# Loading one K tile in four with a transposing DMA in a two-block cached attention kernel

## The chip, the cores and the metric

The kernel runs on one core of a Trainium2 chip. A core has five engines that run their own instruction streams: PE (TensorE, matrix multiply), DVE (VectorE), ACT (ScalarE), POOL (GpSimd) and SP (SyncE, here used only to issue DMAs), and 16 DMA engines that move data between HBM and the on-chip memory. PE writes its results to PSUM; DVE and ACT empty PSUM into SBUF. Engines wait for one another by semaphores.

The metric is the device time of one execution in microseconds.

## The reference

Two independent blocks, A and B, of the same shape; each projects queries, attends over a cache, projects the result, and the two outputs are concatenated:

```python
# B, Sq, D = 16, 64, 640;  H, Sk, Dh = 32, 512, 128;  all bfloat16
q = (x @ wq).reshape(B, Sq, H, Dh).transpose(0, 2, 1, 3)
scores = jnp.einsum("bhqd,bhkd->bhqk", q, k_cache) * (Dh ** -0.5)
p = softmax(scores, axis=-1)
o = jnp.einsum("bhqk,bhkd->bhqd", p, v_cache)
out = o.transpose(0, 2, 1, 3).reshape(B, Sq, H * Dh) @ wo
```

K and V of one batch element and head are 512 x 128 each, 128 KB. Over both blocks they are 134 MB each, and nearly all that the kernel reads.

## The kernel before

**Work units.** A step g is one head for two batch elements: 2 x 64 query rows fill the 128 partitions. A macro m is two neighbouring heads (steps 2m and 2m+1, called sub 0 and 1); there are 256 macros. Index j names the batch element of the pair. Eight macros (16 heads) of one pair form a group; a pass runs all eight pairs through 16 heads of one block, and there are four passes. A chunk is two macros (four heads), the unit of the K and V loads.

**Stages of a macro**, with the names that the code uses:

- KX (PE, L433): eight 128x128 transposes of a K tile (two heads of one j, 2 x 512 keys x 128) into one PSUM bank, KTB. There are two per macro, j = 0 and 1 (KX0, KX1).
- KE (DVE, L442): copies that bank to ktp_ring, in the score matmul's layout. KE0 and KE1 use the same bank, so a KX waits for the KE before it.
- QP2 (PE, L451): queries of two heads; QE2 (ACT, L459) scales and empties them.
- SM2 (PE, L467): four score matmuls, sub by j, into two PSUM banks; it waits for KE1 and for the EX that emptied the banks.
- MX (DVE, L476), EX (ACT, L482): negated row maximum and exponential with row sum, once per sub. RC2 (DVE, L488): reciprocals of the row sums.
- NM (POOL, L496): normalises P into pn_ring, once per sub.
- TR2 (PE, L505): eight transposes of P; TE2 (DVE, L512) empties them.
- PV2 (PE, L524), OE2 (ACT, L532), OP2 (PE, L540 and L545): P times V, emptying, output projection, accumulated over the 16 heads.
- Once per group: XT and XE (PE L604, ACT L612) transpose the next x. The accumulated output goes to outp (OVP, ACT, L555) in the first pass of a block and is added to it (OVF, DVE, L560) in the second; the store follows.

**Order.** The order on each engine is written out as a template per iteration, with an offset that says how many macros ahead each stage works:

```python
PE_T = (("TR2", 1), ("QP2", 4), ("KX", 4, 0), ("SM2", 3), ("PV2", 1), ("XT", 0), ("OP2", 0), ("KX", 4, 1))
DVE_T = (("TE2", 1), ("RC2", 2), ("KE", 4, 0), ("MX", 3, 0), ("MX", 3, 1), ("KE", 4, 1), ("OVF", 0))
POOL_T = (("NM", 0, 0), ("NM", 0, 1))
```

In iteration k, PE thus transposes K of macro k+4, multiplies scores of k+3, transposes P of k+1 and projects the output of k. An engine works strictly in its order. Dependencies are found from what each operation reads and writes; a pruning pass removes waits that another wait implies.

**Loads.** All loads go through SP's queue in one planned order (L229 to L240). Each has a time from which its buffer is free and a due time, in units of iterations; the planner steps through time with an assumed duration of each load (DMA_NS) and always takes the free load with the earliest due time. When the program runs, SP waits at each load for the real semaphore of its buffer. K goes into kn_ring and V into v_ring, both five chunks deep. Per chunk and j there is one K load of 512 KB (L626): 128 partitions, each row of 2 KB holding eight neighbouring keys (t = 8) of one head. V is loaded likewise (L622) with four keys, 1 KB, a row. Weights wq and wo have two buffers by pass, x has one.

Of the kernel before, what the change touches and what calls it, by code (L numbers as in the profile page):

```python
# [5 lines left out]
BF16 = mybir.dt.bfloat16  # L6
# [8 lines left out]
class Cfg:  # L15
    G = 4
    HH = 16
    NKB = 5
# [13 lines left out]
    DVE_T = (("TE2", 1), ("RC2", 2), ("KE", 4, 0), ("MX", 3, 0), ("MX", 3, 1), ("KE", 4, 1), ("OVF", 0))  # L32
    POOL_T = (("NM", 0, 0), ("NM", 0, 1))
    TAIL_SPLIT = 2
    SLOT_NS = 3600.0
    DMA_NS = dict(LDK=3100.0, LDV=3100.0, LDWQ=3900.0, LDWO=4300.0, LDX=700.0)


class Op:
# [3 lines left out]
    def __init__(self, eng, kind, idx, reads=(), writes=(), dur=0.0, ts=None, aux=None):  # L43
        self.eng = eng
        self.kind = kind
        self.idx = idx
        self.reads = tuple(reads)
        self.writes = tuple(writes)
        self.sem = None
        self.count = None  # L50
        self.deps = []
        self.waits = []
        self.dur = dur
        self.ts = ts
        self.aux = aux
        self.dma = kind in ("LDK", "LDV", "LDX", "LDWQ", "LDWO", "ST")


STAGES = ("LDW", "LDX", "LDK", "LDV", "KX0", "KE0", "KX1", "KE1", "QP2", "QE2", "SM2", "MX0", "MX1", "EX0", "EX1",
          "RC2", "NM0", "NM1", "TR2", "TE2", "XT", "XE", "PV2", "OE2", "OP2", "OV", "ST")  # L60
STAGE_IDX = {s: i for i, s in enumerate(STAGES)}
SUB_KINDS = ("KX", "KE", "EX", "NM", "MX")
# [2 lines left out]
def build_plan(dims, cfg):  # L65
# [22 lines left out]

    progs = {e: [] for e in ENGINES}

    def mk(eng, kind, idx, reads, writes, stage, m_ts, sub=0, aux=None, dur=0.0):
        return Op(eng, kind, idx, reads, writes, dur=dur, aux=aux, ts=(m_ts, STAGE_IDX[stage], sub))

# [4 lines left out]
    def make_op(kind, m, sub):  # L98
        g0, g1 = 2 * m, 2 * m + 1
        ps_, bp, grp, h0 = step_info(g0)  # L100
        c = g0 // G
        if kind == "KX":
            return mk("pe", "KX", (m, sub), [("kn", c % cfg.NKB, g0 % G), ("kn", c % cfg.NKB, g1 % G), ("ident",)],
                      [("KTB",)], "KX%d" % sub, m, sub)
        if kind == "KE":
            return mk("dve", "KE", (m, sub), [], [("KTB",), ("ktp", m % cfg.NKT, sub)], "KE%d" % sub, m, sub)
        if kind in ("MX", "EX", "NM"):
            g = 2 * m + sub
            r = g % cfg.NR
            if kind == "MX":  # L110
                return mk("dve", "MX", g, [], [("SB", sub), ("negmax", r)], "MX%d" % sub, m, sub)
            if kind == "EX":
                return mk("act", "EX", g, [("negmax", r)], [("SB", sub), ("p", g % cfg.NP), ("rowsum", r)],
                          "EX%d" % sub, m, sub)
            return mk("pool", "NM", g, [("p", g % cfg.NP), ("recip", r)], [("pn", g % cfg.NPN)], "NM%d" % sub, m, sub)
        r0, r1 = g0 % cfg.NR, g1 % cfg.NR
        if kind in ("XT", "XE"):
            mt = m + cfg.XLEAD
            if mt % MPG != 0 or not (0 <= mt < NMAC):
                return None  # L120
            gq = mt // MPG
            m_ts = mt - cfg.XLEAD + OFF["TR2"]
            if kind == "XT":
                return mk("pe", "XT", gq, [("xn", gq % cfg.NXN), ("ident",)], [("PTB",)], "XT", m_ts, aux=gq)
            return mk("act", "XE", gq, [], [("PTB",), ("xT", gq % cfg.NX)], "XE", m_ts, aux=gq)
        if kind == "QP2":
            return mk("pe", "QP2", m, [("xT", grp % cfg.NX), ("wq", ps_ % 2, h0 // G)], [("QB",)], "QP2", m)
        if kind == "QE2":
            return mk("act", "QE2", m, [], [("QB",), ("qT", m % cfg.NQ)], "QE2", m)
        if kind == "SM2":  # L130
            return mk("pe", "SM2", m, [("qT", m % cfg.NQ), ("ktp", m % cfg.NKT, 0), ("ktp", m % cfg.NKT, 1)],
                      [("SB", 0), ("SB", 1)], "SM2", m)
        if kind == "RC2":
            return mk("dve", "RC2", m, [("rowsum", r0), ("rowsum", r1)], [("recip", r0), ("recip", r1)], "RC2", m)
        if kind == "TR2":
            return mk("pe", "TR2", m, [("pn", g0 % cfg.NPN), ("pn", g1 % cfg.NPN), ("ident",)], [("PTB",)], "TR2", m)
        if kind == "TE2":
            return mk("dve", "TE2", m, [], [("PTB",), ("pT", m % cfg.NT)], "TE2", m)
        if kind == "PV2":
            return mk("pe", "PV2", m, [("pT", m % cfg.NT), ("v", c % cfg.NVB, g0 % G), ("v", c % cfg.NVB, g1 % G)],  # L140
                      [("OB",)], "PV2", m)
        if kind == "OE2":
            return mk("act", "OE2", m, [], [("OB",), ("oT", m % cfg.NO)], "OE2", m)
        if kind == "OP2":
            return mk("pe", "OP2", m, [("oT", m % cfg.NO), ("wo", ps_ % 2, h0 // G)], [("OUTB",)], "OP2", m)
        if kind in ("OV", "OVF", "ST"):
            if h0 + 1 != SPB - 1:
                return None
            last_half = ps_ % NHALF == NHALF - 1
            if kind == "OV":  # L150
                if NHALF == 1:
                    return mk("act", "OV", m, [], [("OUTB",), ("out_sb", grp % 2)], "OV", m, aux=grp)
                if last_half:
                    return None
                return mk("act", "OVP", m, [], [("OUTB",), ("outp", bp)], "OV", m, aux=grp)
            if kind == "OVF":
                if NHALF == 1 or not last_half:
                    return None
                return mk("dve", "OVF", m, [("outp", bp)], [("OUTB",), ("out_sb", grp % 2)], "OV", m, aux=grp)
            if NHALF == 1 or not last_half:  # L160
                return None
            return mk("act", "ST", m, [("out_sb", grp % 2)], [("out_dram", grp)], "ST", m, aux=grp)
        raise ValueError(kind)
# [57 lines left out]
    for c in range(NCHUNK):  # L221
        m0 = MPC * c
        for kind, ring, n_ring, cons, tb in (("LDK", "kn", cfg.NKB, "KX", 2), ("LDV", "v", cfg.NVB, "PV2", 2.5)):
            ready = NEG if c < n_ring else MPC * (c - n_ring + 1) - 1 - OFF[cons]
            for pi, (piece, j, hlo, hhi) in enumerate(chunk_pieces(c)):
                op = mk("sp", kind, (c, j, piece), [], [(ring, c % n_ring, gi) for gi in range(hlo, hhi)], kind,
                        m0, aux=(c, j, hlo, hhi, piece), dur=cfg.DMA_NS[kind] * (hhi - hlo) / 8.0)
                loads.append((ready, m0 - OFF[cons] + 0.01 * hlo, tb + 0.001 * pi, op))
    pending = sorted(loads, key=lambda e: (e[1], e[2]))  # L229
    t_now = min(e[1] for e in loads) - 4.0  # L230
    while pending:
# [12 lines left out]
    def sem_key(op):  # L244
        if op.kind in ("LDK", "LDV"):
            return ("d_" + op.kind[2:].lower(), op.writes[0][1], op.aux[4])
        if op.kind == "LDX":
            return ("d_x", op.writes[0][1])
        if op.kind in ("LDWQ", "LDWO"):
# [97 lines left out]
def mha_kernel(nc, blocks, out, cfg=None):  # L347
# [30 lines left out]
    with contextlib.ExitStack() as es:  # L378
# [7 lines left out]
        outp = sb("outp", [128, NBP, DN], F32) if NHALF > 1 else None  # L386
        xT_ring = sb("xT_ring", [128, NX, KT, 128], BF16)
        xn_ring = sb("xn_ring", [128, NXN, D], BF16)
        kn_ring = sb("kn_ring", [128, NKB, 2, G // 2, 8, DH], BF16)
        v_ring = sb("v_ring", [128, NVB, 2, G, 4, DH], BF16)  # L390
        ktp_ring = sb("ktp_ring", [128, NKT, 2, 2, SK], BF16)
        qT_ring = sb("qT_ring", [128, NQ, 2, 128], BF16)
# [34 lines left out]
        def em_KX(e, op):  # L427
            m, j = op.idx
            g0 = 2 * m
            c, hp = g0 // G, (g0 % G) // 2  # L430
            first = last = None
            for t8 in range(8):
                ins = e.transpose(kt_ps[:, t8, :], kn_ring[:, c % NKB, j, hp, t8, :], ident[:, :])  # L433
                first = first or ins
                last = ins
            return first, last
# [25 lines left out]
        def em_SM2(e, op):  # L462
            m = op.idx
            first = last = None
            for sub in range(2):
                for j in range(2):
                    ins = e.matmul(s_bank(sub)[64 * j:64 * j + 64, :], qT_ring[:, m % NQ, sub, 64 * j:64 * j + 64],  # L467
                                   ktp_ring[:, m % NKT, sub, j, :], start=True, stop=True, tile_position=(0, 64 * j))
                    first = first or ins
                    last = ins  # L470
            return first, last
# [144 lines left out]
        def em_LDKV(e, op):  # L616
# [6 lines left out]
            else:  # L623
                src = blocks[blk][1][2 * bp + j, h0 + hlo:h0 + hhi].rearrange("(hp hs) (p t) d -> (hs p) hp t d",
                                                                              hs=2, t=8)
                ins = e.dma_start(kn_ring[:, c % NKB, j, hlo // 2:hhi // 2], src)  # L626
            return ins, ins

        emitters = dict(KX=em_KX, KE=em_KE, QP2=em_QP2, QE2=em_QE2, SM2=em_SM2, MX=em_MX, EX=em_EX, RC2=em_RC2,
                        NM=em_NM, TR2=em_TR2, TE2=em_TE2, PV2=em_PV2, OE2=em_OE2, OP2=em_OP2, OV=em_OV,  # L630
                        OVP=em_OVP, OVF=em_OVF, ST=em_ST, XT=em_XT, XE=em_XE, INIT1=em_INIT1, INIT2=em_INIT2,
                        LDWQ=em_LDWQ, LDWO=em_LDWO, LDX=em_LDX, LDK=em_LDKV, LDV=em_LDKV)
# [87 lines left out]
```

## Time and profile before

| what | value |
|---|---|
| median of three runs | 959.2 us (958.8 to 959.47) |
| span of the profiled execution | 956.8 us |
| 256 iterations in that span | 3.74 us each, start and end included |
| PE, DVE, ACT, POOL busy | 919.4, 841.9, 567.1, 416.9 us |
| granted PE clock | full (1.00) from 30 us to 900 us |
| read from HBM, written to it | 294.65 MB, 2.62 MB |
| K loads, landing after issue (block A, block B) | 7.0, 4.8 us in the median |

The profiled execution is one run of its own; the profile gives its span, and no total beside it. The three timed runs lie 2.0 to 2.7 us above the span. Busy time of an engine says how long it had an instruction under way; on PE, neighbouring matmuls overlap, so 220 ns for one transpose is its duration and not its cost in a stream. The chain that ended last is followed back from the last instruction: at each step to what released it, or to the instruction before it on its engine. It is the view that tells what ended last, where the busy shares only tell what is close to full.

### The profile page before, as it was taken

Reading aid. Unit: us, or ns where it says so; the run is one execution under the profiler, and the core shown is the slowest. Engines: PE = TensorE matmul, PEld = TensorE weight load, DVE = VectorE, ACT = ScalarE, POOL = GpSimd, SP = SyncE. Lnnn points to the kernel's source line nnn. Section 1 sums busy time; section 2 is a strip of 40 time slices with the busy share of each in tenths; the row PEclk is TensorE's granted clock in tenths of the full one; section 3 lists DMA queues with packets and bytes.
Section 4 is the critical chain, followed back from the end, with each engine's and each line's share of the span. In section 5 each row is a group of like instructions: output and inputs, shape, how many; then the busy total and the mean of one; then the engine's idle time right before and its main releaser. Section 6 shows DMA issues by size and latency. Waiting matters only on the chain.

```text
span 956.8 us, 34351 instructions
## 1 busy us (share of the span) xinstructions
PE 919.4 (96%) x14755; PEld 733.5 (77%) x15008; DVE 841.9 (88%) x1552; ACT 567.1 (59%) x1585; POOL 416.9 (44%) x518
## 2 busy tenths in 40 slices
PE   4999999999999999999999999999999999999997
PEld 3877777778777777877777787777877778777775
DVE  2898899898899999899999899889899998999996
ACT  1666656666665565656566666666666656565654
POOL 0444444444444444444444444444444444444443
PEclk9999999999999999999999999999999999999999
DMA  9999999999999999888999999988888988899830
GB/s 315 364 365 364 351 365 367 365 368 351 338 337 337 343 330 315 299 292 305 322 332 352 326 353 327 306 294 296 302 305 288 308 301 297 295 297 314 295 124 15
DMA packets 230871, 299.51 MB, mean 313 GB/s; under 512 B 9536, under 2 KB 165184, under 8 KB 230720
## 3 DMA queue, kind: packets, MB, share of 16 engines
q1 hardware_dynamic: 228416, 294.69, 91.0%
q8 instruction: 118, 1.93, 0.8%
q10 hardware_dynamic: 2304, 2.62, 0.8%
q14 instruction: 33, 0.27, 0.1%
HBM read 294.65 MB, written 2.62 MB: 311 GB/s over the span
## 4 chain that ended last, share of the span: by engine, by line
PE 89%; DVE 4%; POOL 3%; issue 2%; SPq 1%; DMA 1%; POOLq 0%; DVEq 0%
PE ps L433 22%; PE ps L524 14%; PE ps L451 14%; PE ps L467 14%; PE ps L505 12%; PE ps L545 7%; PE ps L540 5%; POOL pn_ring L496 3%; DVE out_sb L560 1%; DVE ktp_ring L442 1%; DVE pT_ring L512 1%; PE ps L604 1%; DMA xn_ring<-in_A_x_dram 1%; SPq L626 1%; SPq L583 1%
## 5 line engine op out<-in xcount | busy, mean ns | idle before, releaser
L496 POOL TENSOR_SCALAR pn_ring<-p_ring,recip 128x512 bf16<-128x512 bf16 x512 | 416.3, 843 | 532.7 <-DVE recip L488 532.7
L442 DVE COPY ktp_ring<-ps 128x1024 bf16<-128x1024 bf16 x512 | 353.7, 691 | 105.3 <-PE ps L433 85.1
L482 ACT ACTIVATE p_ring<-ps,negmax 128x512 bf16<-128x512 f32 x512 | 345.6, 684 | 4.8 <-DVE negmax L476 4.8
L476 DVE TENSOR_REDUCE negmax<-ps 128x1 f32<-128x512 f32 x512 | 327.3, 681 | 0.4 <-PE ps L467 0.3
L433 PE MATMUL ps<-ident,kn_ring 128*128 128x128 bf16 x4096 | 314.6, 220 | 2.8 <-DMA kn_ring<-in_A_k_cache_dram 1.6
L532 ACT ACTIVATE oT_ring<-ps 128x256 bf16<-128x256 f32 x256 | 98.0, 383 | 306.0 <-PE ps L524 306.0
L433 PEld LDWEIGHTS ps<-ident,kn_ring 128*128 128x128 bf16 x4096 | 251.9, 98 | 34.2 <-DVE ktp_ring L442 2.6
L524 PEld LDWEIGHTS ps<-pT_ring,v_ring 128*128 128x128 bf16 x4096 | 133.5, 98 | 109.2 <-issue 100.0
L451 PE MATMUL ps<-xT_ring,wq_sb 128*128 128x128 bf16 x2560 | 186.4, 220 | 3.2 <-DMA wq_sb<-in_A_wq_dram 3.2
L512 DVE COPY pT_ring<-ps 128x1024 bf16<-128x1024 bf16 x256 | 174.5, 682 | 4.6 <-PE ps L505 3.8
L524 PE MATMUL ps<-pT_ring,v_ring 128*128 128x64 bf16 x4096 | 163.8, 194 | 3.3 <-issue 1.7
L467 PE MATMUL ps<-ktp_ring,qT_ring 128*64 128x512 bf16 x1024 | 159.8, 392 | 0.4 <-ACT p_ring L482 0.4
L505 PE MATMUL ps<-ident,pn_ring 128*128 128x128 bf16 x2048 | 156.7, 219 | 3.5 <-POOL pn_ring L496 3.5
L451 PEld LDWEIGHTS ps<-xT_ring,wq_sb 128*128 128x128 bf16 x2560 | 155.2, 98 | 3.5 <-DMA wq_sb<-in_A_wq_dram 3.5
L459 ACT ACTIVATE qT_ring<-ps 128x256 bf16<-128x256 f32 x256 | 98.4, 384 | 66.8 <-PE ps L451 66.8
L505 PEld LDWEIGHTS ps<-ident,pn_ring 128*128 128x128 bf16 x2048 | 124.1, 98 | 7.0 <-POOL pn_ring L496 6.7
L545 PE MATMUL ps<-wo_sb,oT_ring 128*128 128x128 bf16 x512 | 112.1, 219 | 13.4
L482 ACT ACTIVATION_READ_ACCUMULATOR p_ring<-ps,negmax 128x1 f32 x512 | 105.0, 205 | 0.0
L540 PE MATMUL ps<-wo_sb,oT_ring 128*128 128x512 bf16 x259 | 97.8, 379 | 0.0
L540 PEld LDWEIGHTS ps<-wo_sb,oT_ring 128*128 128x128 bf16 x512 | 50.1, 98 | 30.6 <-ACT oT_ring L532 0.3
L467 PEld LDWEIGHTS ps<-ktp_ring,qT_ring 128*64 128x64 bf16 x1024 | 36.1, 108 | 27.1 <-ACT p_ring L482 0.6
L545 PEld LDWEIGHTS ps<-wo_sb,oT_ring 128*128 128x128 bf16 x512 | 50.1, 98 | 0.0
(13 smaller groups left out, 112.7 us busy)
## 6 DMA issues: line engine op xcount, KB each, us to landing
kn_ring<-in_A_k_cache_dram SPq DMA_DIRECT2D x128, 512.0 KB, 7.0
v_ring<-in_A_v_cache_dram SPq DMA_DIRECT2D x128, 512.0 KB, 7.2
kn_ring<-in_B_k_cache_dram SPq DMA_DIRECT2D x126, 512.0 KB, 4.8
v_ring<-in_B_v_cache_dram SPq DMA_DIRECT2D x126, 512.0 KB, 5.7
wq_sb<-in_A_wq_dram SPq DMA_DIRECT2D x8, 640.0 KB, 10.4
wo_sb<-in_A_wo_dram SPq DMA_DIRECT2D x8, 640.0 KB, 10.2
wq_sb<-in_B_wq_dram SPq DMA_DIRECT2D x8, 640.0 KB, 8.4
wo_sb<-in_B_wo_dram SPq DMA_DIRECT2D x8, 640.0 KB, 7.5
```

The lines of the kernel that those rows point to most:

```text
L433: ins = e.transpose(kt_ps[:, t8, :], kn_ring[:, c % NKB, j, hp, t8, :], ident[:, :])
L442: ins = e.tensor_copy(dst, src)
L451: ins = e.matmul(q_ps[:, sub * 128:(sub + 1) * 128], wq_sb[:, ps_ % 2, kt, hh * DH:(hh + 1) * DH], xT_ring[:, grp % NX, kt, :], start=(kt ...
L467: ins = e.matmul(s_bank(sub)[64 * j:64 * j + 64, :], qT_ring[:, m % NQ, sub, 64 * j:64 * j + 64], ktp_ring[:, m % NKT, sub, j, :], start=T ...
L476: ins = e.reduce_max(negmax[:, r:r + 1], s_bank(g % 2), axis=AX.X, negate=True)
L482: ins = e.activation(p_ring[:, g % NP, :], s_bank(g % 2), ACTF.Exp, bias=negmax[:, r:r + 1], scale=1.0, accum_out=rowsum[:, r:r + 1])
L496: ins = e.tensor_scalar(dst, src, recip[:, r:r + 1], 1.0, ALU.mult, ALU.mult)
L505: ins = e.transpose(pt_ps[:, sub, t, :], pn_ring[:, g % NPN, t * 128:(t + 1) * 128], ident[:, :])
L512: ins = e.tensor_copy(pT_ring[:, m % NT].rearrange("p s t q -> p (s t q)"), pt_ps_flat)
L524: ins = e.matmul(o_ps[:, col:col + 64], v_ring[:, c % NVB, j, gi, t, :], pT_ring[:, m % NT, sub, t, 64 * j:64 * j + 64], start=(t == 0), s ...
L540: ins = e.matmul(out_ps0, oT_ring[:, m % NO, sub, :], wo_sb[:, ps_ % 2, hh, 0:N0], start=(hh == 0), stop=(hh == SPB - 1))
L545: last = e.matmul(out_ps1, oT_ring[:, m % NO, sub, :], wo_sb[:, ps_ % 2, hh, N0:DN], start=(hh == 0), stop=(hh == SPB - 1))
```

## The change

Of the four K tiles of a chunk (two macros, two j), the tile with j = 1 of the second macro, which is the odd one, no longer goes through kn_ring, KX and KE. A transposing DMA (LDKX) reads its 2 x 512 keys x 128 from HBM as 128 rows of 2 KB and writes them, transposed, to a new ring kx_ring of five chunks: partition = head dimension, then t (8), then head and key group (128). The score matmul of odd macros reads that ring for j = 1: for each sub, eight runs of 64 keys instead of one run of 512. The order of the keys is the same as in ktp_ring.

The odd macros' KX1 and KE1 are left out of the templates, and the K load for j = 1 shrinks to the first macro's two heads (256 KB). LDKX is issued on SP's queue; its buffer is free after the SM2 of five chunks before, its due time is one iteration before SM2's, and the planner takes it as 1.7 times as long as a plain load of its size. Its semaphore is one of five, by chunk.

```diff
+    XBAR = True
+    NKX = 5
...
+    def crossed(m, j):
+        return cfg.XBAR and j == 1 and m % MPC == MPC - 1
...
+        if kind in ("KX", "KE") and crossed(m, sub):
+            return None
...
-            return mk("pe", "SM2", m, [("qT", m % cfg.NQ), ("ktp", m % cfg.NKT, 0), ("ktp", m % cfg.NKT, 1)],
+            kt1 = ("kx", c % cfg.NKX) if crossed(m, 1) else ("ktp", m % cfg.NKT, 1)
+            return mk("pe", "SM2", m, [("qT", m % cfg.NQ), ("ktp", m % cfg.NKT, 0), kt1],
                       [("SB", 0), ("SB", 1)], "SM2", m)
...
+                if kind == "LDK" and cfg.XBAR and j == 1:
+                    hhi = min(hhi, G - 2)
+                    if hlo >= hhi:
+                        continue
...
+        if cfg.XBAR:
+            mx = m0 + MPC - 1
+            ready = NEG if c < cfg.NKX else MPC * (c - cfg.NKX + 1) - 1 - OFF["SM2"]
+            op = mk("sp", "LDKX", (c, 1, 0), [], [("kx", c % cfg.NKX)], "LDKX", m0, aux=(c, 1, G - 2, G, 0),
+                    dur=cfg.DMA_NS["LDK"] * 1.7 * 2 / 8.0)
+            loads.append((ready, mx - OFF["SM2"] - 1, 2.7, op))
...
-        kn_ring = sb("kn_ring", [128, NKB, 2, G // 2, 8, DH], BF16)
+        kn_ring = sb("kn_ring", [128, NKB, 3 if cfg.XBAR else 4, 8, DH], BF16)
+        kx_ring = sb("kx_ring", [128, cfg.NKX, 8, 128], BF16) if cfg.XBAR else None
...
+                    kt = ktp_ring[:, m % NKT, sub, j, :]
+                    if cfg.XBAR and j == 1 and m % (G // 2) == G // 2 - 1:
+                        kt = kx_ring[:, (2 * m // G) % cfg.NKX, :, 64 * sub:64 * sub + 64]
...
+        def em_LDKX(e, op):
+            c, j, hlo, hhi, _piece = op.aux
+            blk, bp, grp, ps_, hh0 = step_info(c * G)
+            h0 = (ps_ % NHALF) * HH + hh0
+            src = blocks[blk][1][2 * bp + j, h0 + hlo:h0 + hhi].rearrange("hs (p t) d -> (hs p) (t d)", t=8)
+            ins = e.dma_start_transpose(kx_ring[:, c % cfg.NKX], src)
+            return ins, ins
```

More of the change, by code (lines that the diff above doesn't have):

```diff
@@ L55, in __init__ @@
         self.aux = aux
-        self.dma = kind in ("LDK", "LDV", "LDX", "LDWQ", "LDWO", "ST")
-STAGES = ("LDW", "LDX", "LDK", "LDV", "KX0", "KE0", "KX1", "KE1", "QP2", "QE2", "SM2", "MX0", "MX1", "EX0", "EX1",
+        self.dma = kind in ("LDK", "LDKX", "LDV", "LDX", "LDWQ", "LDWO", "ST")
+STAGES = ("LDW", "LDX", "LDK", "LDKX", "LDV", "KX0", "KE0", "KX1", "KE1", "QP2", "QE2", "SM2", "MX0", "MX1", "EX0", "EX1",
           "RC2", "NM0", "NM1", "TR2", "TE2", "XT", "XE", "PV2", "OE2", "OP2", "OV", "ST")
@@ L246, in sem_key @@
             return ("d_" + op.kind[2:].lower(), op.writes[0][1], op.aux[4])
+        if op.kind == "LDKX":
+            return ("d_kx", op.writes[0][1])
         if op.kind == "LDX":
@@ L432, in em_KX @@
             for t8 in range(8):
-                ins = e.transpose(kt_ps[:, t8, :], kn_ring[:, c % NKB, j, hp, t8, :], ident[:, :])
+                ins = e.transpose(kt_ps[:, t8, :], kn_ring[:, c % NKB, 2 * j + hp, t8, :], ident[:, :])
                 first = first or ins
@@ L466, in em_SM2 @@
                 for j in range(2):
+                    kt = ktp_ring[:, m % NKT, sub, j, :]
+                    if cfg.XBAR and j == 1 and m % (G // 2) == G // 2 - 1:
+                        kt = kx_ring[:, (2 * m // G) % cfg.NKX, :, 64 * sub:64 * sub + 64]
                     ins = e.matmul(s_bank(sub)[64 * j:64 * j + 64, :], qT_ring[:, m % NQ, sub, 64 * j:64 * j + 64],
-                                   ktp_ring[:, m % NKT, sub, j, :], start=True, stop=True, tile_position=(0, 64 * j))
+                                   kt, start=True, stop=True, tile_position=(0, 64 * j))
                     first = first or ins
@@ L625, in em_LDKV @@
                                                                               hs=2, t=8)
-                ins = e.dma_start(kn_ring[:, c % NKB, j, hlo // 2:hhi // 2], src)
+                ins = e.dma_start(kn_ring[:, c % NKB, 2 * j + hlo // 2:2 * j + hhi // 2], src)
             return ins, ins
-        emitters = dict(KX=em_KX, KE=em_KE, QP2=em_QP2, QE2=em_QE2, SM2=em_SM2, MX=em_MX, EX=em_EX, RC2=em_RC2,
+        def em_LDKX(e, op):
[5 more added lines that the diff above has]
+            return ins, ins
+        emitters = dict(LDKX=em_LDKX, KX=em_KX, KE=em_KE, QP2=em_QP2, QE2=em_QE2, SM2=em_SM2, MX=em_MX, EX=em_EX, RC2=em_RC2,
                         NM=em_NM, TR2=em_TR2, TE2=em_TE2, PV2=em_PV2, OE2=em_OE2, OP2=em_OP2, OV=em_OV,
```

## The prediction

> **What bounds the kernel now.** I read the shares of the page first, then the chain of work that ended last, then one repeated stretch of it in order of time, and only then the transfers. Page, busy times; the chain by engine; the DMA queue that carries all loads:
>
> ```profile
> PE 919.4 (96%) x14755; PEld 733.5 (77%) x15008; DVE 841.9 (88%) x1552; ACT 567.1 (59%) x1585; POOL 416.9 (44%) x518
> PE 89%; DVE 4%; POOL 3%; issue 2%; SPq 1%; DMA 1%; POOLq 0%; DVEq 0%
> q1 hardware_dynamic: 228416, 294.69, 91.0%
> ```
>
> PE (TensorE) holds 89% of the chain, so work taken from PE shortens the kernel until something else ends last. Two things stand close behind: DVE (VectorE) at 88%, and the 16 DMA engines at 91%. The chain in order of time, start and length in us:
>
> ```profile
> 401.73 0.45 PE ps L433 x8
> 402.17 0.45 PE ps L505 x8
> ...
> 405.29 0.46 PE ps L433 x8
> ...
> 405.78 0.69 DVE ktp_ring L442
> 406.47 0.73 DVE out_sb L560
> 407.20 0.60 DVE pT_ring L512
> ...
> 407.96 1.63 POOL pn_ring L496 x2
> ...
> 409.64 0.62 PE ps L505 x8
> ```
>
> One eight-fold K transpose (L433) is worth 0.45 us of PE. In the second half of this piece PE is not the bound: DVE empties a K transpose (KE, L442), does the output addition OVF (L560), only then empties the P transposes (TE2, L512); the normalisation NM on POOL (L496) follows, and PE's next P transposes (TR2, L505) wait for it. The same loop in an ordinary iteration (timeline: start, length):
>
> ```profile
> 511.89 0.61 PE L505 MATMUL ps<-ident,pn_ring 128*128 128x128 bf16 x8
> 512.10 0.69 DVE L442 COPY ktp_ring<-ps 128x1024 bf16<-128x1024 bf16 x1 [0.23 <-PE ps L433]
> 512.71 0.68 DVE L512 COPY pT_ring<-ps 128x1024 bf16<-128x1024 bf16 x1
> 513.55 1.63 POOL L496 TENSOR_SCALAR pn_ring<-p_ring,recip 128x512 bf16<-128x512 bf16 x2 [1.94 <-DVE recip L488]
> 515.46 0.61 PE L505 MATMUL ps<-ident,pn_ring 128*128 128x128 bf16 x8
> ```
>
> From TR2 to TR2 is 515.46 - 511.89 = 3.57 us, all PE work. But POOL's second NM ends at 513.55 + 1.63 = 515.18, so the loop TR2, TE2, reciprocal, NM, TR2 would be ready for its next turn only 0.28 us before PE is. The end of the kernel, where no K tile is left to transpose, shows the loop bare and how soon PE follows NM:
>
> ```profile
> 947.16 0.62 PE L505 MATMUL ps<-ident,pn_ring 128*128 128x128 bf16 x8 [0.56 <-POOL pn_ring L496]
> 948.68 1.61 POOL L496 TENSOR_SCALAR pn_ring<-p_ring,recip 128x512 bf16<-128x512 bf16 x2 [1.57 <-DVE recip L488]
> 950.34 0.62 PE L505 MATMUL ps<-ident,pn_ring 128*128 128x128 bf16 x8 [0.56 <-POOL pn_ring L496]
> ```
>
> NM ends at 950.29, TR2 starts at 950.34: 0.05 us later; the bare loop takes 3.18 us. Last, two stretches (columns end in granted clock, DMA share, GB/s) and SP's waits before its DMA issues:
>
> ```profile
> 120.00:240.00 120.00, 118.26 (x1921) 94.66 (x1951) 108.26 (x201) 73.95 (x207) 54.24 (x67) 1.00 1.06 362
> 600.00:720.00 120.00, 118.25 (x1926) 94.76 (x1958) 108.32 (x200) 73.61 (x207) 54.91 (x68) 1.00 0.89 297
> SPq L626 <- PE ps L433: 353.5, 119, 4.0
> SPq L622 <- PE ps L524: 123.4, 81, 2.6
> ```
>
> With weights to prefetch, the queue runs full at 362 GB/s; without them it needs 297. PE is as busy in both, so the full queue costs nothing yet, but its room is small.
>
> **The change part by part.** I count in pairs of iterations: A, whose KX1 and KE1 stay, and B, which loses both. There are 256 iterations, 128 pairs.
>
> Removed from PE: 128 KX by 0.45 us, 57.6 us. By PE alone B would last 3.57 - 0.45 = 3.12 us. The NM loop doesn't allow that: KE1 of the A before still stands ahead of B's TE2 on DVE, as in the row at 512.10, so B's next TR2 starts at 515.18 + 0.05 = 515.23, or 3.34 us after its own. A keeps 3.57: no KE1 stands ahead of its TE2, the loop is near the bare 3.18, and PE ends last. A pair goes from 7.14 to 6.91, a gain of 0.23 us; 128 pairs give 29.4 us. What is late next after B is NM on POOL.
>
> Removed from DVE: 128 KE by 0.69 us, 88 us, hidden behind PE in the ordinary iteration and worth nothing there. It is worth something at the 16 output additions: OVF falls in a B (the last macro of a group is odd), right behind the KE1 that goes. There TR2 to TR2 took 409.64 - 405.58 = 4.06 us (405.58 is that iteration's TR2 in the timeline). With 0.6 to 0.69 us less on DVE the loop is some 3.4 us, below PE's 3.57: 16 x 0.5 = 8 us, of which I take 7.8.
>
> Added waits: the odd SM2 on PE waits for the transposing load's semaphore in place of KE1's. Queued behind it on PE are PV2, OP2 and the next iteration. The load is issued some ten iterations (34 us) ahead, and a K load of 512 KB lands in 4.7 to 8.2 us by the stretch: nothing, while the queue keeps up. If that cover goes, PE waits out the whole lack. On SP the new load waits for the SM2 of five chunks before, one iteration after the K load of its own chunk could go; behind it stand V and K loads that wait for PE still later by the planner's order, so it holds nothing up. One more issue per chunk (0.44 us each, as 0.88 for two) and whatever the transposing issue takes come out of SP's idle 353.5 + 123.4 + 38.8 us (the last for x loads): 4.0 us per pair.
>
> The odd SM2 reads keys in eight runs of 64 instead of one of 512. No row has such a moving operand. Bounds: nothing (as many columns), or two of the four matmuls at double time: in the chain four SM2 matmuls take 0.55 us, 0.14 each, and sixteen of PV2, each 64 columns and an instruction of its own, 0.57, so eight runs of 64 come to 0.28 at the most. That is 0.28 us per pair, in an A, where PE ends last: up to 36 us. I take nothing: PV2's price is that of instructions, and here their number stays.
>
> The transposing transfer, 256 KB, is the open price; call T what it takes of all 16 engines. At least its bytes, 262,144 B at 362 GB/s, 0.72 us: the same bytes through the same engines exclude less. At most I put 1,024 pieces of 256 B (one K row each) at the mean packet of q1: 0.91 x 16 x 956.8 us / 228,416 = 61 ns; over 16 engines, 3.9 us. Between them I use the single packets recorded for q1: 1,024 B took 46 ns in the median and 2,048 B took 84, so 8 ns plus 9.5 per 256 B; a piece 17.5 ns, T = 1.12 us. That is the row nearest to it: packets on the same queue from the same source.
>
> All else that moves is 294.65 + 2.62 - 33.55 = 263.7 MB, or 728.5 us at 362 GB/s. With 10 us of beginning and end (my estimate from the last V pieces, which land in 3 us, and two iterations) the transfers need 738.5 + 128 T. For T = 1.12 that is 882 us, below the engines' sum: hidden. It becomes the bound at T = 1.43 and equals the span of before at 1.70.
>
> One rule speaks against the change. Row first: a 128x128 block on PE takes 0.45 / 8 = 0.056 us of PE time. The Trainium skill (VectorE: DVE Perf Modes, The three transpose paths) gives 390 ns on TensorE and 1309 ns by the DMA for such a block, and its Rules for kernel authors prefer TensorE where PSUM will do. By it, as an estimate, eight blocks one after another would make T 10.5 us and the time about 2,080 us. PE's row here is seven times below the page's price, so the page does not price work in a stream; the DMA's price is in no row here.
>
> Sum, against the profiled execution: span 956.8 - 29.4 - 7.8 + 2 (four starting pairs without gain, 0.9, and about 1 for the first transfers) = 921.6 us. The median of the runs is 2.4 us above the span, so 924.
>
> **The rivals.**
>
> DMA becomes the bound (slower): in its place PE waits at SM2 and KX for loads. For it: the share stands at 1.06 in the second eighth of the span, and a transfer of another kind goes into the same queue. Against: later only 297 of 362 GB/s are needed. From T = 1.70 on it is slower; T = 2.25 gives 1026.5 + 2.4 = 1029 us.
>
> Block by block (slower by far): T near the upper end 3.9 gives 738.5 + 499 + 2.4 = 1240 us. For it: no row here shows data turned on their way. Against: nothing but the packet line. The Trainium skill's price (VectorE: DVE Perf Modes, The three transpose paths) would put it further out still.
>
> DMA bound, yet faster: T from 1.43 to 1.70 gives 924 to 959 us.
>
> The strided SM2 eats the gain: 924 + 36 = 960, no change.
>
> PE alone ends last: if B's loop shrinks to the bare 3.18, a pair is 6.75 and the gain 50 + 8 us: about 903 us.
>
> **How the numbers follow.** Chances: forecast 0.41, mild DMA bound 0.10, PE alone 0.03: faster 0.54. No change 0.05. DMA bound up to T = 2.25 0.22, beyond 0.19: slower 0.41. (0.2%, 1.9 us, is about what a measurement here can tell.) The forecast's own range is 918 to 934, by 0.05 us more or less per pair; leaving out the last case, 0.19, the range is 903 to 1030.
>
> **What would show it.** KX and KE x384 in place of x512; PE near 862 us busy, DVE near 754; TR2 waiting for NM in about half the iterations, pairs of 6.91 us; OVF off the chain. Wrong it would be if PE's waits name the transposing load, if SP stops waiting for PE and its transposing issue is long, or if landings grow past 30 us.

## The result and the profile after

The changed kernel takes 1010.98 us in the median (1009.42 to 1011.95) against 959.04 us before: a ratio of 1.0537, with a 95% interval of 1.0522 to 1.0552. It is slower by 5.4%, where a gain of 3.7% had been forecast. The profiled execution took 1011.2 us, its span is 1009.4.

Lines move with the change: KX is L454, KE L463, SM2 L491, NM L520, TR2 L529, TE2 L536, the plain K and V loads are L650 and L646, and the transposing load is L658. Page of the changed kernel: busy times, the chain by engine, the loads' queue.

```profile
PE 916.3 (91%) x13984; PEld 678.4 (67%) x13984; DVE 767.1 (76%) x1424; ACT 565.7 (56%) x1585; POOL 417.5 (41%) x518
SPq 55%; DMA 18%; PE 15%; POOL 5%; DVE 4%; issue 3%; ACT 0%; POOLq 0%; DVEq 0%
q1 hardware_dynamic: 347184, 294.70, 110.9%
```

PE has 89% of the chain before and 15% after. SP's queue and the DMA engines have 73% in its place. The queue moves the same 294.7 MB, but in 347,184 packets, and their time grows from 91% to 110.9% of 16 engines' span. The two stretches that were shown of before (last columns: granted clock, DMA share, GB/s), and SP's waits before its issues:

```profile
120.00:240.00 120.00, 112.25 (x1754) 83.77 (x1752) 94.53 (x176) 71.48 (x203) 52.10 (x64) 1.00 1.14 299
600.00:720.00 120.00, 113.90 (x1772) 84.40 (x1771) 95.77 (x179) 72.22 (x202) 53.19 (x66) 1.00 1.15 294
SPq L650 <- PE ps L454: 16.6, 27, 1.4
SPq L646 <- PE ps L548: 7.6, 15, 1.0
```

In these stretches the queue is full (1.14 and 1.15 of the engines' time) and carries 299 and 294 GB/s, where it carried 362 in the first of them before. SP hardly waits for PE any more: 24 us in place of 477. PE waits for loads instead; its K transposes in all 46.5 us directly:

```profile
PE ps L454 <- DMA kn_ring<-in_B_k_cache_dram: 26.0, 38, 2.1
PE ps L454 <- DMA kn_ring<-in_A_k_cache_dram: 20.5, 29, 2.2
```

SP's queue in order of time shows the new issue beside the old ones (start, length in us):

```profile
606.14 3.77 SPq L658 DMA_TRANSPOSE kx_ring<-in_B_k_cache_dram  x1
609.96 2.14 SPq L650 DMA_DIRECT2D kn_ring<-in_B_k_cache_dram  x2
612.14 1.92 SPq L646 DMA_DIRECT2D v_ring<-in_B_v_cache_dram  x2
```

Three explanations fit this: the transposing transfer costs the DMA engines more than was reckoned; its issue blocks SP; or the engines' gain isn't there and the queue only looks full. The first has three forms: a price per transfer, per byte, or from something outside the transfer.

### The profile page after: what moved, and what is told of

It is laid out like the page before. It is cut to its first block, busy times and chain, and to the rows that moved or that the text cites. A ratio compares the mean times of both kernels' runs of the same rounds, so it can differ in the third digit from the quotient of the medians.

```text
span 1009.4 us, 32695 instructions
## 1 busy us (share of the span) xinstructions
PE 916.3 (91%) x13984; PEld 678.4 (67%) x13984; DVE 767.1 (76%) x1424; ACT 565.7 (56%) x1585; POOL 417.5 (41%) x518
## 3 DMA queue, kind: packets, MB, share of 16 engines
q1 hardware_dynamic: 347184, 294.70, 110.9%
q8 instruction: 111, 1.82, 0.7%
HBM read 261.10 MB, written 2.62 MB: 261 GB/s over the span
## 4 chain that ended last, share of the span: by engine, by line
SPq 55%; DMA 18%; PE 15%; POOL 5%; DVE 4%; issue 3%; ACT 0%; POOLq 0%; DVEq 0%
SPq L658 31%; SPq L646 12%; SPq L650 10%; DMA kn_ring<-in_B_k_cache_dram 9%; DMA kn_ring<-in_A_k_cache_dram 7%; POOL pn_ring L520 5%; PE ps L454 5%; PE ps L548 2%; PE ps L491 2%; SPq L621 2%; PE ps L529 2%; DVE ktp_ring L463 2%; DVE pT_ring L536 2%; PE ps L472 2%; PE ps L564 2%
## 5 line engine op out<-in xcount | busy, mean ns | idle before, releaser
L520 POOL TENSOR_SCALAR pn_ring<-p_ring,recip 128x512 bf16<-128x512 bf16 x512 | 416.8, 843 | 584.7 <-DVE recip L512 584.7
L463 DVE COPY ktp_ring<-ps 128x1024 bf16<-128x1024 bf16 x384 | 265.7, 692 | 171.2 <-PE ps L454 159.1
L454 PE MATMUL ps<-ident,kn_ring 128*128 128x128 bf16 x3072 | 238.0, 221 | 47.6 <-DMA kn_ring<-in_B_k_cache_dram 26.0
L454 PEld LDWEIGHTS ps<-ident,kn_ring 128*128 128x128 bf16 x3072 | 188.8, 99 | 74.4 <-issue 56.2
L536 DVE COPY pT_ring<-ps 128x1024 bf16<-128x1024 bf16 x256 | 175.6, 686 | 61.0 <-PE ps L529 61.0
L564 PE MATMUL ps<-wo_sb,oT_ring 128*128 128x512 bf16 x512 | 168.0, 382 | 3.3 <-DMA wo_sb<-in_B_wo_dram 2.1
L529 PE MATMUL ps<-ident,pn_ring 128*128 128x128 bf16 x2048 | 157.8, 220 | 7.1 <-POOL pn_ring L520 0.8
L491 PE MATMUL ps<-ktp_ring,qT_ring 128*64 128x512 bf16 x768 | 162.0, 397 | 1.2 <-ACT p_ring L506 1.2
L529 PEld LDWEIGHTS ps<-ident,pn_ring 128*128 128x128 bf16 x2048 | 120.1, 98 | 47.7 <-POOL pn_ring L520 46.5
L491 PE MATMUL ps<-kx_ring,qT_ring 128*64 128x512 bf16 x256 | 81.4, 400 | 0.0
L564 PEld LDWEIGHTS ps<-wo_sb,oT_ring 128*128 128x128 bf16 x512 | 50.4, 98 | 35.5 <-DMA wo_sb<-in_B_wo_dram 2.3
L491 PEld LDWEIGHTS ps<-ktp_ring,qT_ring 128*64 128x64 bf16 x768 | 35.9, 108 | 28.7 <-ACT p_ring L506 1.8
```

What stands on the lines that cost most here:

```text
L454: ins = e.transpose(kt_ps[:, t8, :], kn_ring[:, c % NKB, 2 * j + hp, t8, :], ident[:, :])
L463: ins = e.tensor_copy(dst, src)
L520: ins = e.tensor_scalar(dst, src, recip[:, r:r + 1], 1.0, ALU.mult, ALU.mult)
L529: ins = e.transpose(pt_ps[:, sub, t, :], pn_ring[:, g % NPN, t * 128:(t + 1) * 128], ident[:, :])
L536: ins = e.tensor_copy(pT_ring[:, m % NT].rearrange("p s t q -> p (s t q)"), pt_ps_flat)
L564: ins = e.matmul(out_ps0, oT_ring[:, m % NO, sub, :], wo_sb[:, ps_ % 2, hh, 0:N0], start=(hh == 0), stop=(hh == SPB - 1))
```

## The experiments

**The transposing alone.** The same kernel with the new load as a plain copy, which leaves the tile unturned:

```diff
-            ins = e.dma_start_transpose(kx_ring[:, c % cfg.NKX], src)
+            ins = e.dma_start(kx_ring[:, c % cfg.NKX], src.rearrange("q (t d) -> q t d", t=8))
```

> The changed kernel, but the new load copies its 256 KB into kx_ring as a plain DMA, without turning it: the odd macros' second key tile is wrong data, and everything else (order, waits, strided score matmul, KX and KE left out) stays. If the transposing transfer's price is the whole loss, the engines' sum of the prediction must now show: about 924 us, 918 to 930. If the gain on the engines was never there (a slower strided score matmul, or another loop), 940 to 960 or more.

Measured: 920.51 us (919.8 to 921.33), a ratio of 0.9603 (0.9587 to 0.9619) to the kernel before, span 918.0. So the whole loss, 90 us, is the price of turning the data, and the engines' gain is there. The timeline of this kernel shows the pair as it was reckoned (TR2 is L529, NM L520):

```profile
500.74 0.62 PE L529 MATMUL ps<-ident,pn_ring 128*128 128x128 bf16 x8
504.32 0.61 PE L529 MATMUL ps<-ident,pn_ring 128*128 128x128 bf16 x8
504.52 0.69 DVE L463 COPY ktp_ring<-ps 128x1024 bf16<-128x1024 bf16 x1 [0.23 <-PE ps L454]
505.13 0.68 DVE L536 COPY pT_ring<-ps 128x1024 bf16<-128x1024 bf16 x1
505.97 1.62 POOL L520 TENSOR_SCALAR pn_ring<-p_ring,recip 128x512 bf16<-128x512 bf16 x2 [2.09 <-DVE recip L512]
507.65 0.62 PE L529 MATMUL ps<-ident,pn_ring 128*128 128x128 bf16 x8
```

TR2 to TR2 is 3.58 us and then 3.33, a pair of 6.91. In the second, KE (504.52) still stands ahead of TE2 (505.13), and TR2 starts 0.06 us after NM. Over the whole run TR2's weight load waits for NM 129 times, in half of the 256 iterations (us in total, times, longest):

```profile
PEld ps L529 <- POOL pn_ring L520: 49.8, 129, 0.9
```

**Size and number of the transfers.** One transposing DMA of 128 rows as two of 64, and, the other way, two tiles in one DMA of 256 rows (the j = 1 tiles of both macros of every second chunk, written where their plain copies would lie):

```diff
-            ins = e.dma_start_transpose(kx_ring[:, c % cfg.NKX], src)
+            for hs in range(2):
+                ins = e.dma_start_transpose(kx_ring[:, c % cfg.NKX, :, 64 * hs:64 * hs + 64], src[64 * hs:64 * hs + 64, :])
...
```

```diff
-        return cfg.XBAR and j == 1 and m % MPC == MPC - 1
+        return cfg.XBAR and j == 1 and (m // MPC) % 2 == 1
...
+        kx_ring = [kn_ring[:, i, 2:4].rearrange("p a t d -> p (a t d)").rearrange("p (t r) -> p t r", t=8) for i in range(NKB)]
```

> Each transposing DMA of 128 source rows is split into two of 64 rows; bytes and pieces stay. Theory S, every transposing DMA makes the 16 DMA engines stand once for about 1.4 us whatever its size (the long packet seen once per engine and transfer): 128 more such stops, by 0.96 us (what the span of the changed kernel leaves for one) to 1.46 us (what the packets show): 1130 to 1200 us. Theory P, the price goes with the bytes or pieces: 1000 to 1020, as the changed kernel. Theory Q, the time of issuing on SP's queue bounds and goes with the descriptors: as P.

> The same number of turned K tiles, but two per DMA: in every second chunk both macros' j = 1 tiles come by one transposing DMA of 256 rows (512 KB), 64 DMAs in place of 128; the other chunks are as in the kernel before. Theory S (one stop per DMA): 64 stops fewer, 1009 - 61 to 1009 - 93 = 916 to 948 of span, so 916 to 952 us, with the engines' own pace at about 914 below it. Theory P (price by bytes or pieces, two stops in the longer transfer): 1000 to 1015.

Measured: 1024.16 us for the split (one run, span 1022.4), 994.06 us (993.32 to 995.21) for the double. Theory S is far off: twice the DMAs cost 13 us, not 120 to 190; half the DMAs gain 17, not 60 to 90. Theory P misses by only 4 us (1000 to 1020) and 6 us (1000 to 1015); it is the experiment with fewer instructions, below, that speaks against it.

The records of single packets tell more. A transposing DMA of 128 rows runs as 1,024 pieces of 256 B, each 18 ns in the median. In most transfers some 20 pieces are far longer, 1.3 us in the mean: they begin some 0.48 us after the first piece, and in the median stop they end within 0.04 us of one another. This is one such transfer of the changed kernel. Each column counts the packets that begin in the 0.1 us from the time at its head, and leaves out every second 0.1 us:

```
us from first piece     -0.2  0.1  0.3  0.5  0.7  0.9  1.1  1.3  1.5  1.7  1.9  2.1
256 B pieces               0   99  100    1    0    0    7    7    4    7  106  115
1,024 B plain packets     34    4    5    5    4    5    2    2    1    0    0    0
```

While the others stand, 1,024 B packets of the V load before still begin, some 4 to 5 per 0.1 us where 16 engines begin 34: in this transfer two engines are late. (The records don't name the engine; this is worked out from the rate.) When the last of them has come up, all go on. The usual stop has one late engine. From 0.1 to 0.4 us after the first piece one engine would begin 6 such packets; two or more begin in 96 of the 110 stops, 6 or 7 in 63 of them, and none begins in the 18 transfers without a stop. So a transposing DMA brings the 16 engines into step and waits for the latest. The split DMA's second half, which follows on the first, almost never stops: 6 of 128, against 109 of the 128 first halves.

What makes an engine late? Queue q8 brings instructions: 111 packets of 16 KB in the changed kernel, 1.09 us each, no two of them at the same time. The table counts, in the packet records, the transfers with a stop (five or more pieces over 0.3 us), and whether a 16 KB packet had begun since the transfer before (from 0.3 us after its first piece to 0.3 us after this one's):

```
kernel               transfers  stops   with a fetch: stopped   without: stopped
changed                 128      110        107 of 109               3 of 19
split in two            256      115        107 of 109               8 of 147
two tiles in one         64       64         63 of 63                1 of 1
```

The last row tells nothing of the cause, as nearly every transfer there has a fetch; in those DMAs the long pieces end just when SP's issuing instruction does (last section). Of the 14 stops in the changed kernel in which fewer than two V packets begin in the 0.3 us, 13 have the 16 KB packet itself under way; the other is the kernel's first transfer. In the transfer shown only one fetch had begun since the one before, so what made its second engine late isn't shown.

That is the new theory F: the price is 64 pieces of 18 ns, 1.15 us, and beside that the lateness from instruction fetches, 111 x 1.09 us in all. It gives 738.5 + 147 + 121 = 1006 us against a span of 1009.4. (An unstopped transfer takes 0.96 us from first to last piece; with that for 1.15 the sum is 982, and some 27 us are left over that no run accounts for.)

**Fewer fetches, with the DMA work left alone.** Nearly all fetched instructions are PE's: the kernel with fewer of them, below, has 10,240 PE instructions and 41 packets of 16 KB less than the changed one, some 66 B an instruction, and at that price the 13,984 matmuls and as many weight loads make up all of q8's 1.82 MB. So one kernel keeps only the first matmul of each sum; the other, its control, keeps every matmul as an instruction but makes those after the first 2 columns wide:

```diff
-                for kt in range(KT):
+                for kt in range(1):
...
-                    for t in range(4):
+                    for t in range(1):
```

```diff
...
+                    w = 128 if kt == 0 else 2
+                    ins = e.matmul(q_ps[:, sub * 128:sub * 128 + w], wq_sb[:, ps_ % 2, kt, hh * DH:(hh + 1) * DH],
+                                   xT_ring[:, grp % NX, kt, 0:w], start=(kt == 0), stop=(kt == KT - 1))
...
+                        w = 64 if t == 0 else 2
...
```

> The changed kernel with fewer PE instructions: of each sum over blocks in the query projection and in P times V only the first matmul is left (queries from one fifth of x, outputs from one quarter of the keys); loads, waits and transposing DMAs stay. PE then has some 17,400 matmuls and weight loads in place of 27,970, so some 68 instruction fetches of 16 KB in place of 111. Theory F, a transposing DMA stops 15 engines until the one that a fetch of 1.09 us has made late comes up: 738.5 + 128 x 1.15 + 68 x 1.09 = 960, 945 to 972 us. Theory X, every transposing DMA stops the engines for a reason of its own: 1000 to 1012, since the DMA engines are the bound and their work is the same.

> The control for the kernel with fewer PE instructions: every matmul of the query projection and of P times V is kept as an instruction, but all after the first of each sum are 2 columns wide (so most of each sum is left out). PE's time falls about as there, its instruction count and the fetches (111) stay. Theory F: 1000 to 1012 us, nothing gained. If it is PE's lighter load that helps there and not the fetches, this one comes out equally fast.

Measured: 961.13 us (960.13 to 962.83) with fewer instructions, 1009.92 us (two runs, 1009.17 and 1010.67) in the control. Their pages, first the kernel with fewer instructions, busy times, the two queues and the chain:

```profile
PE 757.5 (79%) x8864; PEld 483.4 (50%) x8864; DVE 754.7 (79%) x1424; ACT 568.0 (59%) x1585; POOL 414.6 (43%) x518
q1 hardware_dynamic: 347184, 294.70, 110.3%
q8 instruction: 70, 1.15, 0.5%
SPq 56%; DMA 22%; PE 9%; POOL 5%; DVE 5%; issue 3%; POOLq 0%; DVEq 0%
```

and the control:

```profile
PE 877.7 (87%) x13984; PEld 627.6 (62%) x13984; DVE 767.4 (76%) x1424; ACT 555.2 (55%) x1585; POOL 416.0 (41%) x518
q1 hardware_dynamic: 347184, 294.70, 110.9%
q8 instruction: 111, 1.82, 0.7%
SPq 64%; DMA 19%; PE 9%; issue 3%; POOL 3%; DVE 2%; POOLq 0%; DVEq 0%
```

The loads' queue has the same packets and bytes in both. The control's PE did not become as light as its partner's (39 us less than in the changed kernel, against 159), but PE has 9% of the chain in both, so it bounds neither; the control gains 1 us. 41 fetches fewer are worth 48.7 us of span, 1.19 each. Spread over 16 engines, their 1.09 us each would be 2.8 us in all; the time falls as if all 16 waited out every one. This carries theory F; a stop that belongs to the transfer, or a price by its bytes or pieces, would have left both at 1010. The control has 112 stops, the light kernel 82: 67 of 70 transfers with a fetch and 15 of 58 without, so some have another cause. That 960 was foretold for the light kernel so closely is worth less than the difference of the two, since the sum leaves the 27 us above open.

**The other queue.** V's loads on ACT's queue:

```diff
+                op = mk("act" if kind == "LDV" and c >= n_ring else "sp", kind, (c, j, piece), [], [(ring, c % n_ring, gi) for gi in range(hlo, hhi)], kind,
...
+        if op.kind == "OE2" and op.idx in act_v:
+            acts.extend(act_v.pop(op.idx))
```

> The changed kernel with V's loads, after the first five chunks, issued from ACT's queue behind the OE2 that tells that the V buffer is free; the transposing loads and all else stay on SP. If the 16 engines themselves stand while a transposing DMA stops (theory S, engines), nothing changes: 1000 to 1015. If SP's issuing of the transposing DMA (3 to 6 us each) is what holds the plain loads back (theory Q), or only the one queue stands and another can use the engines meanwhile, the time falls to 925 to 960; the packets' times then tell these two apart.

Measured: 1226.35 us (one run), far worse than any theory said. SP has 248 V loads fewer to issue, and its issuing is not what bounds this kernel, for it now waits for PE before the transposing loads, 401.7 us in 84 waits, as it never did in the changed kernel. The transposing loads now take 16.7 us in the median to land, in place of 8.6, and a transfer that stops stretches over 6.5 us in place of 2.4. Two readings are left, and no run tells them apart: that two queues put the engines further out of step, or that K loads come late because they stand on SP behind a transposing load that waits for PE (PE's K transposes wait 150.7 us for them, in place of 46.5). This stays open.

**Two transfers in a row.** Moving the even chunk's transposing DMA to just ahead of the odd one's:

```diff
+    sp = [o for o in progs["sp"] if not (o.kind == "LDKX" and o.aux[0] % 2 == 0)]
+    held = {o.aux[0] + 1: o for o in progs["sp"] if o.kind == "LDKX" and o.aux[0] % 2 == 0}
+    progs["sp"] = [x for o in sp for x in ((held[o.aux[0]], o) if o.kind == "LDKX" else (o,))]
```

> The changed kernel with the transposing DMAs of two chunks issued one behind the other on SP's queue, every second chunk; nothing else differs. Theory F: the second of two finds the engines already in step and stops only if a fetch falls between: about 64 to 70 stops in place of 110, 738.5 + 147 + 64 x 1.2 = 962 to 975 us; up to 995 if 128 blocks in a row make the engines wait for SP's issuing, as the one long transfer of 256 rows did. Theory X: 1005 to 1015.

Measured: 1016.61 us (one run), the time that theory X had named and not theory F's. The stops fall only to 87, and the held load comes late; PE now waits for it at SM2, 68.8 us in all:

```profile
PE ps L495 <- DMA kx_ring<-in_B_k_cache_dram: 36.0, 17, 5.1
PE ps L495 <- DMA kx_ring<-in_A_k_cache_dram: 32.8, 17, 4.6
```

So the time decides nothing between F and X, since stops and late loads moved against each other. The stops still go with the fetches: counted as above, 84 of 93 transfers with a fetch stopped and 3 of 35 without.

**A smaller dose.** If each transposing DMA costs the queue more than a plain load and spares the engines something, there is a dose at which both end together. These kernels take the transposing load only in some chunks, and write its tile where the plain one would lie, so memory and ring depth are those of before:

```diff
-        return cfg.XBAR and j == 1 and m % MPC == MPC - 1
+        return cfg.XBAR and j == 1 and m % MPC == MPC - 1 and (m // MPC) % 2 == 0
...
+            ins = e.dma_start_transpose(kn_ring[:, c % NKB, 3], src)
```

> Half the dose: the transposing load only in every second chunk (one K tile in eight, 64 DMAs; the turned tile lies in the place of kn_ring that the plain one would take, so the memory and ring depth are those of before). Engines: 956.8 - 18.6 + 1 = 939 of span. DMA, by theory F with a stop at nearly every one (1.7 fetches between two): 774.8 + 10 + 64 x (1.15 + 1.2) = 935. So 941 us, 936 to 952: faster than before. If the price of a transposing DMA grew with the time since the last one beyond that (3 us or more), 985 and up.

> One transposing DMA in four chunks (32), in the chunks whose KE1 would stand right before the 16 output additions on DVE. Engines: 32 x 0.23 = 7.4 us from the pairs and 7.8 from the additions, 956.8 - 15.2 + 1 = 942.6 of span, 944.5 us. DMA with a stop each, at the 2.6 us per transfer that the half dose leaves: 798.9 + 10 + 32 x 2.6 = 892, no bound. By theory F and the engines' sum 941 to 948 us. If the additions are worth nothing: 952.

> Three transposing DMAs in eight chunks (48), the same chunks and as many odd ones between. Engines: 48 x 0.23 + 7.8 = 18.8, so 939 of span, 941 us; DMA 787 + 10 + 48 x 2.6 = 922, close below. 939 to 948 us.

> Half the dose again (64), but in the odd chunks, which hold the 16 additions, where the first half dose took the even ones, which don't. Engines: 64 x 0.23 + 7.8 = 22.5, 935 of span, 937 us; DMA as in the first half dose, which ended at 950.7 of span with the queue full. If the queue was that kernel's bound, 948 to 954 again; if its engines were, with the additions missing, 937 to 945.

Each ratio is to runs of before that were taken with it (medians 958.45 to 959.04).

| dose | transfers | expected us | measured us | ratio to before (95%) |
|---|---|---|---|---|
| none (before) | 0 | | 958.87 | |
| a quarter, chunks 1 of 4 | 32 | 944.5 (941 to 948) | 944.46 | 0.9846 (0.9831 to 0.9861) |
| three eighths | 48 | 941 (939 to 948) | 941.31 | 0.9816 (0.9799 to 0.9832) |
| half, odd chunks | 64 | 948 to 954 or 937 to 945 | 950.24 | 0.9921 (0.9894 to 0.9949) |
| half, even chunks | 64 | 941 (936 to 952) | 951.03 | 0.9920 (0.9903 to 0.9936) |
| all (the change) | 128 | 924 (918 to 934) | 1010.98 | 1.0537 (1.0522 to 1.0552) |

Three eighths is the fastest of these doses: 1.8% faster than before and 6.9% faster than the change; the quarter is 3 us behind it, and their runs don't overlap. The half dose in even chunks came out at the upper end of its range: theory F's sum for the queue was 935 us of span, the profiled run's is 950.7, which leaves 2.6 us a transfer in place of the 2.35 assumed. All 64 transfers stop there. The chain's shares by engine and SP's largest wait for PE, first at three eighths:

```profile
PE 79%; POOL 8%; DVE 7%; issue 2%; SPq 2%; DMA 1%; ACT 0%; POOLq 0%; DVEq 0%
SPq L653 <- PE ps L457: 81.2, 65, 3.6
```

then at the half dose in odd chunks (here the profiled run is the slowest of six, 956.8 us):

```profile
PE 55%; SPq 17%; DMA 12%; POOL 7%; DVE 5%; issue 3%; POOLq 0%; DVEq 0%
SPq L653 <- PE ps L457: 26.0, 46, 1.6
```

At three eighths PE ends last and SP still waits for it; at the half SP and the DMA engines have 29% of the chain, and PE 55%. Both halves end at the same time although one has the 16 output additions among its chunks and the other not, so there the queue, not the engines' own pace, sets the time.

## Why the prediction was wrong

- **The engines' part held.** 921.6 us of span were reckoned, the plain copy gives 918.0. B's iteration is bound by NM at 3.33 us (3.34 reckoned), A stays at 3.58, a pair is 6.91, and TR2 waits for NM in 129 iterations. The additions' 7.8 us are in the quarter dose, which met 944.5 and would have been 952 without. (The busy times named as signs were not met even in the plain copy: PE 879.1 and DVE 765.1 us, in place of 862 and 754.)
- **The strided SM2 was rightly put at nothing:** with eight runs of 64 a score matmul took 400 ns on the page, with one run of 512 it took 397.
- **The step that failed is T = 1.12 us, "what it takes of all 16 engines".** The pieces were sized well: 17.5 ns reckoned, 18 measured. The term leaves out that one transfer needs all 16 engines at once. By 738.5 + 128 T = 1009.4, T was 2.12 us; 0.97 more than 64 pieces of 18 ns, against 111/128 x 1.09 = 0.95 from fetches (with an unstopped transfer's 0.96 us for the pieces, 0.2 us of T stays unexplained). T is no fixed price either: the half dose leaves 2.6. So the transfers became the bound, and PE waited for loads that the prediction took as hidden. The measured time lies in the rival "DMA becomes the bound", up to T = 2.25 and 1029 us, which had a chance of 0.22 where the forecast had 0.41; its reason, a transfer of another kind in a queue with little room, was right, but it did not name the waiting for the latest engine. A row that bore on it, the instruction queue's 118 packets in 0.8% of the engines' time (one microsecond each), stood on the page of before and was not put into the sum:

```profile
q8 instruction: 118, 1.93, 0.8%
```

- **SP's room was rightly judged as no bound, but not by its figure.** The 4.0 us per pair were not idle any more: the transposing issue took 1.9 to 6.1 us, and SP spent 960 of the 1009 us in issuing. That the full queue stretches the issues, and their own length is not the bound, shows in the kernel with fewer PE instructions, where the same issues take 910 us.
- **Two of the signs of being wrong came, two did not.** SP stopped waiting for PE and its transposing issue was long; but PE's waits name the plain K loads, which stand behind the transposing ones in the queue, and the transposing loads land in 8.6 us, not past 30.
- **The block-by-block rival and the price in the Trainium skill.** Without a stop, a transfer of eight 128x128 blocks runs from first to last piece in 0.96 us, 0.12 us a block; with a stop it takes 2.40 us. The Trainium skill (VectorE: DVE Perf Modes, The three transpose paths) gives 1309 ns for one block; in a stream the trace disagrees with it by a factor of four to eleven. The Trainium skill (DMA: Bandwidth & Descriptors, Latency and other measured facts) gives 261 GB/s for a transposing DMA with a non-contiguous middle dimension in one kernel, and some 350 to 400 GB/s for the contiguous case. Here 262,144 B in 0.96 us are 273 GB/s without a stop, and 109 GB/s with one; no run tells which of the two cases this load is, and with a stop the trace is far below both.

## What to carry to other kernels

Before a transposing DMA goes into a busy queue, look at what makes single DMA engines late, the instruction queue first: here a load that needed all 16 engines in step paid for the latest, while plain loads ran at 362 GB/s beside as many fetches. Price such a change by testing its parts apart: the plain copy of the same bytes gave the engines' gain in one experiment, and so the room that the transfer may take. And where two bounds stand close, look for the dose: three eighths of the change was worth 1.8%, all of it cost 5.4%.

## What the runs showed of the hardware

- In a transposing DMA of 256 KB the engines that were ahead stood for some 1.3 us until the latest came up, in 110 of 128 cases; in 107 of these a 16 KB instruction fetch (1.09 us) had begun since the transfer before.
- In the DMA of 256 rows the long pieces ended 0.05 us (median of 64) after SP's issuing instruction did, and it stretched over 3.7 us; in the DMAs of 128 rows the issue had ended 3.6 us before. Why the longer one waits for its issue was not tried.
- The shortest issue of a transposing DMA held SP for 1.2 us with 64 rows (split in two) and 1.4 with 128 (the control); that of a plain K load for 0.33 (before).
- With V's loads on a second queue beside the transposing one the kernel took 1226 us in place of 1011; the cause is open.
- The page's count of bytes read from HBM falls from 294.65 to 261.10 MB in the changed kernel, by just the 33.55 MB that the transposing DMAs move; they are not in that count.
